# A block-sparse attention and SwiGLU kernel: queries loaded for both halves of the rows, constant masks, other landing times and ranks in its planner

## The chip, the core and the metric

One core of a Trainium2 chip runs the kernel. The engines named here are TensorE (PE, matmuls; PEld its weight loads), VectorE (DVE), ScalarE (ACT), GpSimd (POOL) and SyncE (SP), which only issues transfers. The metric is the time of one execution in microseconds (us) on the device; lower is better. A table of runs gives a median and its extremes, and one execution was profiled.

## What is computed

Attention over blocks of 32 positions, where a block sees its two neighbours, itself, the first and the last block and three sampled ones, and the first and last block see all. Its output, rows of 8 heads x 64, goes through a SwiGLU feed-forward network (FFN).

```python
B, H, S, D = 4, 8, 768, 64          # 24 blocks of 32
scores = (1 / sqrt(D)) * q @ k.T
mask = (abs(blk_i - blk_j) <= 1) | (blk_i == 0) | (blk_j == 0) | (blk_i == 23) | (blk_j == 23)
mask |= "kb in sampled_blocks[qb]"  # 3 sampled blocks for every block of queries
scores = where(mask, scores, -1e9)
attn = softmax(scores)              # exp(s - max) / (sum + 1e-9)
x = (attn @ v).transpose(0, 2, 1, 3).reshape(3072, 512)
g, val = x @ w_gate, x @ w_val      # 512 -> 1536
out = (g * sigmoid(g) * val) @ w_out  # 1536 -> 512
```

All tensors are fp32. q and k are drawn with a standard deviation of about 0.4, v with 0.1.

## The kernel before

**Tiling.** The 3072 rows are eight chunks of 384 rows, two for each batch: chunk 2b holds blocks 1 to 12 of batch b, chunk 2b+1 blocks 0, 23 and 13 to 22. A chunk has three tiles of 128 rows (four blocks). For every chunk come the attention blocks, then the FFN: 24 groups of 12 gate and value matmuls (p, L1462) and 12 groups of 9 for the output (po, L1508).

**Precision.** Chunk 0 is computed in fp32 while the weights are still on their way. From chunk 1 on, each fp32 operand is scaled by a power of two and split into two fp16 parts, high and low (ScalarE's L380, VectorE's L383), and a product is the sum of three fp16 products (two loops over high and low for the scores). The power of two comes from the sum of squares: ScalarE squares with a running sum (L391), TensorE adds over partitions, VectorE does the exponent arithmetic (pow2, L373 to L377).

**A block** (function `block`): scores qk (L1170) into PSUM, from the keys of its window (kst) and copied keys (kring, L1142); the masked maximum `top` (L682) on VectorE, exponentials (L1187 to L1190) on ScalarE, reciprocal, high and low half of the normalised weights pp (L380, L383), a transposing transfer to pts (L1215) issued by SyncE, and the product with v (L1229). `full_rows` does blocks 0 and 23 against all keys (qkf L962, pvf L1029).

**The queries** (function `load_q`). The host's qT holds each tile's queries as 128 rows, of which rows 64 to 127 are a copy of rows 0 to 63; a row holds 8 heads x 128 positions. A tile is loaded by two transfers of 64 rows (L881, on POOL's queue for batches 1 to 3, on SyncE's for batch 0), each taking every second head, so 128 partitions hold each head once. They are squared (L391), the norm is summed (nrm_q, L896), the high and low halves are written beside the raw tile in the staging buffer (`two`), and four transfers inside the chip (`spread`, L906, SyncE) write both halves into qs, so that each head is there for both halves of the partitions.

**Scales and masks.** The factor on the scores is (key scale) x (query scale) x 1/8. Since the scores in PSUM are still scaled, each tile makes three factors (es, L1095 to L1097) and a mask of its own, msk = dup x (a large negative number in the tile's scale), L1099. `top` adds it; dup counts duplicate key blocks.

**The order.** A `Plan` holds every step as a task: engine, its time in us, what it needs, the buffers it takes and uses, and for a step that issues transfers their time (`dma`). `order` is a list scheduler over a modelled clock: on each free engine it takes the waiting task with the lowest rank whose buffers are free. A transfer starts DMA_HEAD after its issue, queues behind others, and is taken to have landed DMA_TAIL after its end and no earlier than DMA_LATE after its issuing step. RANKS, a table of two bytes for each task, sets the ranks. The engines then run the steps in the planned order and wait on semaphores for what they need, so the plan sets the order and the chip the times. Rings of buffers: staging 4, qs 2, pp, pts and e 3 each, qk and pv 2 each in PSUM, FFN 4 in PSUM, keys kst 1.

```python
                if t.dma is not None:
                    start = max(queue.get(eng, 0.0), now + DMA_HEAD)
                    both = sum(max(0.0, q - start) if eng == "SP" else min(t.dma, max(0.0, q - start)) for e, q in queue.items() if e != eng)
                    queue[eng] = start + t.dma + both
                    t.end = max(queue[eng] + DMA_TAIL, t.end + DMA_LATE)
```

## Time and profile before

| what | value |
|---|---|
| median of 3 runs | 886.74 us |
| lowest, highest | 876.78, 895.16 us |
| the profiled execution, its own time | 888.1 us |
| its span (first to last instruction) | 886.3 us |
| mean granted TensorE clock | 0.940 |
| TensorE busy | 785.5 us (89%) |
| VectorE busy | 569.4 us (64%) |
| ScalarE busy | 513.2 us (58%) |
| GpSimd busy | 264.4 us (30%) |
| moved by transfers | 138.38 MB, 156 GB/s |

The page cuts the span into 40 equal slices of 22 us; a digit is a tenth of busy time, PEclk the granted clock in tenths.

```profile
PE   5778963599998959799799999999699999999998
DVE  6647868898897736667467657675477647851220
PEclk9878985889999889999999999999799999999999
DMA  8997879868564997669968786689959553652001
```

In the first ten slices VectorE is busy and TensorE has gaps; then TensorE is nearly always busy until the end. Transfers are nearly always under way up to the last tenth. A row of a group gives line, engine, operation, output and inputs, the count, busy time and mean time of one, and idle time of the engine ahead of it with what ended most of that. In the other views a row starts with a time from the span's start.

### The profile page before, as it was taken

The page shows a single profiled execution, that of the slowest core. Times are in us where ns is not written, and L with a number is a line of the kernel's source. Part 1 is how long each engine was busy: PE and PEld are TensorE (multiplying, and loading weights), DVE is VectorE, ACT ScalarE, POOL GpSimd, SP SyncE. Part 2 cuts the span into 40 slices and gives each one's busy share as a digit, 9 for nine tenths or more (in the row PEclk, how much of TensorE's full clock was granted, in tenths as well). Part 3 has the DMA queues.
Part 4 walks back from the last instruction along what each step waited for, and adds up shares of the span by engine and source line. Part 5 has one row for each costly group of instructions (what it writes and reads, how often), then busy time and mean ns, then how long its engine had stood idle before and what let it go on. Part 6 is the DMA issues. An engine that isn't in the chain of part 4 may idle for free.

```text
span 886.3 us, 24339 instructions
## 1 busy us (share of the span) xinstructions
PE 785.5 (89%) x9436; PEld 466.2 (53%) x9436; DVE 569.4 (64%) x1855; ACT 513.2 (58%) x1260; POOL 264.4 (30%) x371
## 2 busy tenths in 40 slices
PE   5778963599998959799799999999699999999998
PEld 4665542354565525465355646654366556655653
DVE  6647868898897736667467657675477647851220
ACT  4756465766688635578357556675366647652220
POOL 3423234561134312334124322332123311320220
PEclk9878985889999889999999999999799999999999
DMA  8997879868564997669968786689959553652001
GB/s 228 211 228 224 202 131 284 226 206 193 110 145 143 221 179 156 138 157 228 201 157 148 137 171 137 158 218 160 174 130 179 121 150 59 138 118 39 1 1 36
DMA packets 178083, 138.38 MB, mean 156 GB/s; under 512 B 138480, under 2 KB 141680, under 8 KB 177968
## 3 DMA queue, kind: packets, MB, share of 16 engines
q1 hardware_dynamic: 162704, 92.78, 49.6%
q0 software_dynamic: 11680, 37.76, 17.9%
q10 hardware_dynamic: 3584, 6.29, 2.4%
q8 instruction: 74, 1.21, 0.6%
q14 instruction: 41, 0.34, 0.1%
HBM read 80.68 MB, written 12.58 MB: 105 GB/s over the span
## 4 chain that ended last, share of the span: by engine, by line
PE 68%; DMA 20%; DVE 7%; issue 2%; ACT 1%; SPq 1%; POOL 0%; DVEq 0%; POOLq 0%; ACTq 0%
PE p L1462 33%; PE po L1508 14%; DMA pts<-pp 4%; PE qk L1170 4%; PE pv L1229 4%; PE po L1385 4%; PE p L1329 3%; DMA ptsf<-ppf 3%; DMA qs<-qraw 2%; DMA kst<-k 2%; DMA w1raw<-in_w_dram 2%; DMA w<-in_v_dram 1%; DVE w L413 1%; PE p L1339 1%; PE qkf L962 1%
## 5 line engine op out<-in xcount | busy, mean ns | idle before, releaser
L1462 PE MATMUL p<-xt,w 128*128 128x384 f16 x2016 | 344.4, 330 | 2.0 <-ACT xt L1245 1.4
L1462 PEld LDWEIGHTS <-w 128*128 128x128 f16 x2016 | 194.3, 99 | 135.6 <-issue 10.7
L1508 PE MATMUL po<-w,h 128*128 128x512 f16 x756 | 172.1, 384 | 0.0
L1483 POOL TENSOR_TENSOR h<-act,h 128x384 f16<-128x384 f32 x84 | 80.4, 960 | 269.4 <-ACT h L1480 269.0
L1151 POOL DMA_INDIRECT vring<-vd,vidx x76 | 74.5, 981 | 182.4 <-PE pv L1229 130.5
L1508 PEld LDWEIGHTS <-h 128*128 128x128 f16 x756 | 72.1, 99 | 94.7 <-issue 13.9
L1190 ACT ACTIVATE e<-e,nb,es 128x256 f32<-128x256 f32 x152 | 90.0, 593 | 2.5
L1466 ACT ACTIVATE act<-p,gsc 128x384 f32<-128x384 f32 x84 | 48.1, 576 | 60.2 <-PE p L1462 36.4
L383 DVE SCALAR_TENSOR_TENSOR pp<-e,rr,pp 128x256 f16<-128x256 f32 x152 | 72.1, 519 | 9.0 <-ACT pp L380 7.8
L380 ACT ACTIVATE pp<-e,rr 128x256 f16<-128x256 f32 x152 | 67.4, 498 | 17.8 <-DMA pts<-pp 11.0
L1469 DVE SCALAR_TENSOR_TENSOR act<-act,p 128x384 f32<-128x384 f32 x84 | 46.1, 548 | 47.8 <-ACT act L1466 45.5
L1229 PE MATMUL pv<-pts,vring 128*64 128x32 f16 (+1 forms) x2432 | 53.2, 194 | 22.1 <-DMA pts<-pp 16.7
L1480 ACT CAST h<-act 128x384 f16<-128x384 f32 x84 | 42.1, 506 | 51.4 <-DVE act L1472 51.1
L1229 PEld LDWEIGHTS <-vring 128*64 128x64 f16 x2432 | 48.0, 116 | 39.5 <-issue 33.1
L1472 DVE SCALAR_TENSOR_TENSOR act<-act,hs,p 128x384 f32<-128x384 f32 x84 | 51.3, 612 | 23.8 <-PE p L1462 21.4
L682 DVE CUSTOM_DVE_ANT_1 e<-qk,msk 128x256 f32<-128x256 f32 x152 | 57.2, 418 | 9.4 <-PE qk L1170 9.4
L1170 PEld LDWEIGHTS <-qs 128*32 128x32 f16 x2432 | 36.9, 102 | 32.7 <-issue 24.8
L1170 PE MATMUL qk<-kring,qs 128*32 128x160 f16 x1216 | 43.2, 248 | 6.0 <-DVE kring L1142 6.0
L1170 PE MATMUL qk<-kst,qs 128*32 128x96 f16 x1216 | 39.8, 218 | 9.3 <-ACT ef L984 3.8
L1142 DVE COPY kring<-kst 128x256 f16 x198 | 36.7, 245 | 7.9 <-PE qk L1170 6.7
L881 POOL DMA_DIRECT2D qraw<-in_q_dram x36 | 23.2, 648 | 52.3 <-DMA qs<-qraw 31.2
L1400 ACT ACTIVATE ot<-po,oc 128x512 f32<-128x512 f32 x21 | 14.3, 680 | 41.1 <-PE po L1508 41.1
(195 smaller groups left out, 1129.8 us busy)
## 6 DMA issues: line engine op xcount, KB each, us to landing
vring<-vd SPq DMA_DIRECT2D x76, 192.0 KB
w1raw<-in_w_dram SPq DMA_DIRECT2D x24, 512.0 KB
qs<-qraw SPq DMA_DIRECT2D x84, 128.0 KB
vfull<-vd POOLq DMA_DIRECT2D x12, 512.0 KB
w2raw<-in_w_dram SPq DMA_DIRECT2D x12, 512.0 KB
out_dram<-ot ACTq DMA_DIRECT2D x20, 256.0 KB
qraw<-in_q_dram POOLq DMA_DIRECT2D x36, 128.0 KB
kraw<-in_k_dram POOLq DMA_DIRECT2D x9, 512.0 KB
```

What stands on the lines that cost most here:

```text
L380: nc.scalar.activation(hi, src, AF.Copy, scale=scale)
L383: nc.vector.scalar_tensor_tensor(lo, src, scale, hi, op0=ALU.mult, op1=ALU.subtract)
L682: nc.vector.tensor_tensor_reduce(ev[:, g], stv[:, g], msk.unsqueeze(2).broadcast_to([P, 8, BLK]), scale=scale, scalar=-3.0e38 if scale > 0 ...
L1151: nc.gpsimd.indirect_dma_start(vf[0:96, 1, :], None, bt.vd, bass.IndirectOffsetOnAxis(ap=vidx[0:96, qb : qb + 1], axis=0))
L1170: nc.tensor.matmul(stv[u * BLK : (u + 1) * BLK, g, sl].rearrange("p s k -> p (s k)"), o.q[:, l, h // 2, h % 2, col : col + BLK], keys_of(h ...
L1190: nc.scalar.activation(ev[:, g], ev[:, g], AF.Exp, bias=nb_[:, g : g + 1], scale=o.es[:, 0:1], accum_out=c["rs"][:, g : g + 1],)
L1229: nc.tensor.matmul(pvv[hh * D : (hh + 1) * D, n % 2, j, 0 : 2 - l], vg[:, cc, l, 2 * j + hh, :], pq[:, g, 0 : 2 - l, cc, u, :], start=cc = ...
L1462: nc.tensor.matmul(t[:, 0:T], w_[:, f, m, k_, :], xt.tile[:, l, k_, :], start=i == 0, stop=i == 11)
L1466: nc.scalar.activation(get(act, f"act_{ci}_{f}"), pg.tile[:, 0:T], AF.Tanh, scale=c["gsc"][:, f : f + 1])
L1472: nc.vector.scalar_tensor_tensor(act.tile, act.tile, c["hs"][:, 1:2], pw.tile[:, 0:T], op0=ALU.mult, op1=ALU.mult)
L1483: nc.gpsimd.tensor_tensor(hv()[:, 1, :], act.tile, hv()[:, 0, :], op=ALU.subtract)
L1508: nc.tensor.matmul(po.tile, hv[:, l, ts_], wo16[:, f, m, :], start=f == 0 and i == 0, stop=f == NF - 1 and i == 2)
```

## The change

One load of 128 rows x 1024 columns (512 KB) brings a query tile, the copy of the rows too, so that both halves of the partitions hold all eight heads. The square runs on 64 rows of 1024 columns, since the other 64 are the same numbers; the high and low halves are made for all 128 rows and written straight into qs, and no transfer spreads them. So the square now takes the qs buffer, and its ScalarE output is a part of qs that is overwritten later.

The mask no longer has the tile's scale: -(2^100) x min(dup, 1), made once at the start. `top` waits for that constant, and the exponential for the tile's scale. The keys' scale is stored with factors of 1/8 and -1/8, and a tile's es is one instruction.

In the planner, transfers are taken to land later (DMA_TAIL, DMA_LATE and several `dma` times), a batch's loads of keys and values wait for the load two before and not one, and the table of ranks is another.

```diff
-DMA_HEAD, DMA_TAIL, DMA_LATE = 1.0, 0.5, 1.35
+DMA_HEAD, DMA_TAIL, DMA_LATE = 1.0, 1.6, 2.2
...
 RANKS = """
-    IETuJBIk6kKSJb4mySPIL0M1fjSfNBshHDi0NJ8kFCSMKsYmSS+nIrgqUjO5JIow8CwaGepHEzHvJ1ICXyOBFWMcvhL8NdUeGCNBODMyfinqA5
+    BbJbrbiv6LrBrIqtdK3nrhSzrrcQqunElqxOsJOjeLkokrF7k61zuo2oRrAwrOqyy6xlqseSmp8pr5ujNqk4op+lHHjqskurj7k+s++eXKnJos
...
-        "qs": (work, [P, 2, 2, 4, P], F16, 2),
+        "qs": (work, [P, 2, 4, 2, P], F16, 2),
...
-        v_.tensor_scalar(dup, dup, 1.0, None, op0=ALU.min)
-        v_.tensor_scalar(dupm, dup, -(2.0 ** 100), None, op0=ALU.mult)
+        v_.tensor_scalar(dupm, dup, 1.0, -(2.0 ** 100), op0=ALU.min, op1=ALU.mult)
...
-            loads.append(add("POOL" if b else "SP", 0.75 if b else 0.42, load, need + (loads[-1:] if b else []), rank, ...
+            loads.append(add("POOL" if b else "SP", 0.75 if b else 0.42, load, need + (loads[-2:-1] if b else []), rank, ...
...
-            sc["s"] = small_t([P, 2], f"{what}s", f"{what}s_{b}", 2)
+            sc["s"] = small_t([P, 4], f"{what}s", f"{what}s_{b}", 2)
             pow2(m, sc["s"][:, 0:1], sc["s"][:, 1:2], 1, f"{what}{b}", 0 if what == "k" else 8)
+            if what == "k":
+                for i, x in enumerate((0.125, -0.125)):
+                    nc.vector.tensor_scalar(sc["s"][:, 2 + i : 3 + i], sc["s"][:, 1:2], x, None, op0=ALU.mult)
...
-                                    use=pi + ([] if f0 else [bt.ks]), dma=1.25))
+                                    use=pi + ([] if f0 else [bt.ks]), dma=1.5 if b else 2.5))
...
         def load():
-            raw = get(st, f"qraw_{si}")[:, 0:512]
-            for hh in range(2):
-                sl = slice(hh * D, (hh + 1) * D)
-                (nc.gpsimd if b else nc.sync).dma_start(
-                    raw[sl, :].rearrange("p (j q) -> p j q", j=4),
-                    qT[b, sub, sl, :].rearrange("p (j t q) -> p t j q", j=4, t=2)[:, hh],
-                )
-
-        def two():
-            return st.tile.bitcast(F16)[:, 1024:2048].rearrange("p (l n) -> p l n", l=2)
+            (nc.gpsimd if b else nc.sync).dma_start(get(st, f"qraw_{si}"), qT[b, sub])
+
+        def part(l):
+            return o.q[:, l].rearrange("p j t q -> p (j t q)")
 
         def square():
+            o.q = get(qs, f"qs_{si}")
             o.acc = small_t([P, 1], "qacc", f"qacc_{si}")
-            sumsq(st.tile[:, 0:512], o.acc, two()[:, 0, :])
+            nc.scalar.activation(part(0)[0:D].bitcast(BF16), st.tile[0:D], AF.Square, accum_out=o.acc[0:D])
...
-        def spread():
-            q_ = get(qs, f"qs_{si}")
-            for hh in range(2):
-                for to in range(2):
-                    nc.sync.dma_start(
-                        q_[to * D : (to + 1) * D, hh].rearrange("p l j q -> p (l j q)"),
-                        two()[hh * D : (hh + 1) * D].rearrange("p l n -> p (l n)"),
-                    )
-
-            o.q = q_.rearrange("p t l j q -> p l j t q")
-
-        t = add("POOL" if b else "SP", 1.3 if b else 1.25, load, need, rank, take=[st], dma=1.4, behind=...)
+        t = add("POOL" if b else "SP", 0.75 if b else 0.4, load, need, rank, take=[st], dma=1.7, behind=...)
         q_load.append(t)
-        t = add("ACT", 0.66, square, [t], rank, use=[st])
+        t = add("ACT", 1.15, square, [t], rank, take=[qs], use=[st])
         t = add("PE", 0.1, norm, [t], rank, take=[n])
         o.scaled = add("DVE", 0.6, scale, [t], NORM, use=[n])
-        t = add("ACT", 0.72, lambda: hi_part(two()[:, 0, :], st.tile[:, 0:512], o.siq[:, 0:1]), [o.scaled], rank, use=[st])
-        t = add("DVE", 0.75, lambda: lo_part(two()[:, 1, :], st.tile[:, 0:512], o.siq[:, 0:1], two()[:, 0, :]), [t], rank, use=[st])
-        o.done = add("SP", 2.45, spread, [t], rank, take=[qs], use=[st], dma=2.45)
+        t = add("ACT", 1.15, lambda: hi_part(part(0), st.tile, o.siq[:, 0:1]), [o.scaled], rank, use=[st, qs])
+        o.done = add("DVE", 1.3, lambda: lo_part(part(1), st.tile, o.siq[:, 0:1], part(0)), [t], rank, use=[st, qs])
...
-            def scale(o=o, si=si, sparse=sparse):
-                o.es = small_t([P, 3], "es", f"es_{si}")
-                nc.vector.tensor_scalar(o.es[:, 0:1], bt.ksc["s"][:, 1:2], o.siq[:, 1:2], 0.125, op0=ALU.mult, op1=ALU.mult)
-                nc.vector.tensor_scalar(o.es[:, 2:3], bt.ksc["s"][:, 1:2], o.siq[:, 1:2], -0.125, op0=ALU.mult, op1=ALU.mult)
-                nc.vector.tensor_scalar(o.es[:, 1:2], bt.ksc["s"][:, 0:1], o.siq[:, 0:1], -8e9, op0=ALU.mult, op1=ALU.mult)
-                o.msk = small_t([P, 4, 8], "msk", f"msk_{si}", 4)
-                nc.vector.tensor_scalar(
-                    o.msk[:, 0 : len(sparse), :], dup[:, sparse[0] : sparse[-1] + 1, :], o.es[:, 1:2], None, op0=ALU.mult
-                )
-
-            tsc = add("DVE", 0.85, scale, [o.scaled, bt.ksc_t, t_dup], r0)
+            def scale(o=o, si=si):
+                o.es = small_t([P, 2], "es", f"es_{si}")
+                nc.vector.tensor_scalar(o.es, bt.ksc["s"][:, 2:4], o.siq[:, 1:2], None, op0=ALU.mult)
+
+            tsc = add("DVE", 0.2, scale, [o.scaled, bt.ksc_t], r0)
...
-        vl = add("SP", 1.2 if new else 0.45, values, bt.v_done + v_read[slot], rank, dma=1.05)
+        vl = add("SP", 1.2 if new else 0.45, values, bt.v_done + v_read[slot], rank, dma=1.9 if new else 1.15)
...
-        a = in_turn("top", "DVE", 0.75, top, [a, tsc, full_exp[0]], rank, take=[e], use=[qk])
-        a = in_turn("exp", "ACT", 1.5, power, [a], rank, use=[e])
+        a = in_turn("top", "DVE", 0.75, top, [a, t_dup, full_exp[0]], rank, take=[e], use=[qk])
+        a = in_turn("exp", "ACT", 1.5, power, [a, tsc], rank, use=[e])
...
-        a = add("SP", 1.27, turn, [a], rank, take=[pts], use=[pp], dma=1.35)
+        a = add("SP", 1.27, turn, [a], rank, take=[pts], use=[pp], dma=1.5)
```

In the full rows the tile's es takes the place of a factor of their own (esf, L946).

How the order moves is shown at three places. A row is a line of the kernel, an operation, its output and its inputs (the number at a name's end counts the buffers handed out), its shape, and how many alike follow one another. Lines of the changed kernel are about 25 lower: L380 is L378 there, L391 L389 or L889, L1187 L1162, L1190 L1165, L1215 L1190, L1142 L1117, L1462 L1437.

First, ScalarE ahead of chunk 1's feed-forward part. w are the weights being squared and split, e and pp a block's exponentials and normalised weights (the number after the name is the block), act_0 is chunk 0's first gate.

```order
L380 ACTIVATE pp_17_2464<-e_17_2031,rr_17_2424 128x256 x2
L380 ACTIVATE pp_18_2471<-e_18_2083,rr_18_2278 128x256 x2
L391 ACTIVATE wsq_2_2478,oacc<-w_99 128x512
L1245 CAST xt_120<-pv_15_2153 128x4x64
L1187 ACTIVATE nb_20_2495<-mx_20_2486,es_2285 128x2
L1190 ACTIVATE e_20_2485,rs_20_2494<-e_20_2485,nb_20_2495,es_2285 128x256 x2
L380 ACTIVATE w_97<-w_97,wsc 128x512
L380 ACTIVATE w_98<-w_98,wsc 128x512
L458 CAST w_97<-w_97 128x512
L1343 ACTIVATE act_0_2563<-p_0_2334,gsc_2516 128x384
```

Before, blocks 17 to 20 stand among the weights and ahead of chunk 0's gates. After the change the same blocks stand here:

```order
L1162 ACTIVATE nb_17_2586<-mx_17_2570,es_1403 128x2
L1165 ACTIVATE e_17_2569,rs_17_2585<-e_17_2569,nb_17_2586,es_1403 128x256 x2
L1162 ACTIVATE nb_18_2700<-mx_18_2626,es_1403 128x2
L1165 ACTIVATE e_18_2625,rs_18_2699<-e_18_2625,nb_18_2700,es_1403 128x256 x2
L378 ACTIVATE pp_17_2748<-e_17_2569,rr_17_2739 128x256 x2
L1162 ACTIVATE nb_19_2790<-mx_19_2745,es_2214 128x2
L1165 ACTIVATE e_19_2744,rs_19_2789<-e_19_2744,nb_19_2790,es_2214 128x256 x2
L389 ACTIVATE k_1_0_2527,kacc_2803<-kraw_0_2524 128x2x512
L378 ACTIVATE pp_18_2874<-e_18_2625,rr_18_2751 128x256 x2
L889 ACTIVATE qs_2879,qacc_2880<-qraw_2227 64x1024
```

The blocks follow one another, with squares of keys and queries of batch 1 between them; chunk 0's gates stand ahead of them all.

Second, SyncE's queue in the first half of batch 1, before. pts are the transposing transfers, vring the values of a block's window.

```order
L1215 DMA_TRANSPOSE pts_7_4569<-pp_7_4488 128x8x128
L1148 DMA vring_112<-vd_114 96x1024
L1215 DMA_TRANSPOSE pts_8_4646<-pp_8_4560 128x8x128
L906 DMA qs_4697<-qraw_3770 64x1024 x4
L1215 DMA_TRANSPOSE pts_9_4787<-pp_9_4654 128x8x128
L1148 DMA vring_110<-vd_114 96x1024
L1148 DMA vring_111<-vd_114 96x1024
L1215 DMA_TRANSPOSE pts_10_4856<-pp_10_4735 128x8x128
```

The same place after the change:

```order
L1190 DMA_TRANSPOSE pts_7_4603<-pp_7_4540 128x8x128
L1123 DMA vring_112<-vd_114 96x1024
L1190 DMA_TRANSPOSE pts_8_4623<-pp_8_4564 128x8x128
L1190 DMA_TRANSPOSE pts_9_4754<-pp_9_4625 128x8x128
L1123 DMA vring_110<-vd_114 96x1024
L1123 DMA vring_111<-vd_114 96x1024
L1190 DMA_TRANSPOSE pts_10_4862<-pp_10_4820 128x8x128
```

Only the four spreading transfers between the blocks 8 and 9 are gone.

Third, VectorE where batch 3's keys come in. es and msk are the scale and mask of the first query tile, kring the copied keys of a block, hs the normalisation of the feed-forward part of the chunk before.

```order
L1096 TENSOR_SCALAR es_10884<-ks_10536,siq_10870 128x1
L1097 TENSOR_SCALAR es_10884<-ks_10536,siq_10870 128x1
L1099 TENSOR_SCALAR msk_10888<-dup,es_10884 128x32
L383 SCALAR_TENSOR_TENSOR qraw_10655<-qraw_10655,siq_10870 128x512
L1139 COPY kring_108<-kst_10651 128x8x32
L1140 COPY kring_108<-kst_10651 128x8x32
L1142 ISA
L1142 COPY kring_108<-kst_10651 128x8x32
```

Twelve rows later comes the first row of the normalisation (L1435, hs). After the change:

```order
L1410 TENSOR_REDUCE hs_10766<-xn_10748 128x1
L1412 TENSOR_SCALAR hs_10766<-hs_10766 128x1
L1413 TENSOR_SCALAR hs_10766<-hs_10766 128x1
L1414 TENSOR_SCALAR hs_10766<-hs_10766 128x1
L1417 TENSOR_SCALAR gsc_10771<-wsc,vs_6102 128x12
L1419 SCALAR_TENSOR_TENSOR oc_10773<-vs_6102,hs_10766 128x1
L1471 SCALAR_TENSOR_TENSOR oc_10773<-oc_10773,osc 128x1
L1444 SCALAR_TENSOR_TENSOR act_0_10776<-act_0_10776,p_0_10716 128x384
L1447 SCALAR_TENSOR_TENSOR act_0_10776<-act_0_10776,hs_10766,p_0_10734 128x384
L1444 SCALAR_TENSOR_TENSOR act_1_10791<-act_1_10791,p_1_10753 128x384
L1447 SCALAR_TENSOR_TENSOR act_1_10791<-act_1_10791,hs_10766,p_1_10778 128x384
L1114 COPY kring_107<-kst_10551 128x8x32
```

The copies of keys now stand behind the normalisation and the first two gates of that feed-forward part.

On TensorE the list has 16,822 rows after the change and 16,825 before, on VectorE 1,927 and 1,988, on ScalarE 818 in both, on GpSimd 394 and 393, and on SyncE 303 and 323.

More of the change, by code (lines that the diff above doesn't have):

```diff
@@ L564, in load @@
                 (nc.gpsimd if b else nc.sync).dma_start(raws[i][1](), src[b, i * 256 : (i + 1) * 256, :].rearrange("(t p) n -> p t n", p=P))
-            loads.append(add("POOL" if b else "SP", 0.75 if b else 0.42, load, need + (loads[-1:] if b else []), rank, behind=loads[0] if i else None, take=[] if i else bufs + parts[:1],
+            loads.append(add("POOL" if b else "SP", 0.75 if b else 0.42, load, need + (loads[-2:-1] if b else []), rank, behind=loads[0] if i else None, take=[] if i else bufs + parts[:1],
                              use=[buf] if i and b else [], dma=2.1 if b else 1.6))
@@ L648, in put @@
                     )
-                done.append(add("SP", 0.43, put, los, rank, use=parts[i : i + 1], dma=1.45))
+                done.append(add("SP", 0.43, put, los, rank, use=parts[i : i + 1], dma=1.55))
             bt.all_lo += los
@@ L942, in full_rows @@
                           use=vbuf[i : i + 1] if i else [], dma=1.85))
-        def scale():
-            es[0] = small_t([P, 1], "esf", f"esf_{b}")
-            nc.vector.tensor_scalar(es[0], bt.ksc["s"][:, 1:2], o.siq[:, 1:2], 0.125, op0=ALU.mult, op1=ALU.mult)
-        tsc = add("DVE", 0.2, scale, [bt.ksc_t, o.scaled], rank)
         pvs = []
@@ L1181, in top @@
             c["mx"] = small_t([P, 2], "mx", f"mx_{nq}")
-            masked_top(ev, qk.tile.rearrange("p (g s k) -> p g s k", g=2, k=BLK), o.msk[:, n, :], c["mx"])
+            masked_top(ev, qk.tile.rearrange("p (g s k) -> p g s k", g=2, k=BLK), dupm[:, qb, :], c["mx"])
         def power():
```

155 lines of the change are left out of this document (77 added, 78 removed).

## The prediction

> **What bounds the kernel now.** I read the page's span and the shares of the chain that ended last first, then the table of four stretches, then the waits of TensorE.
>
> ```profile
> span 886.3 us, 24339 instructions
> PE 68%; DMA 20%; DVE 7%; issue 2%; ACT 1%; SPq 1%; POOL 0%; DVEq 0%; POOLq 0%; ACTq 0%
> core 0: us, PE busy (x) PEld busy (x) DVE busy (x) ACT busy (x) POOL busy (x), PEclk, DMA share, GB/s
> 0.00:76.00 76.00, 52.66 (x897) 44.99 (x897) 48.27 (x172) 48.15 (x137) 29.49 (x73) 0.87 1.02 230
> 76.00:232.30 156.30, 121.80 (x1113) 68.78 (x1114) 126.52 (x330) 97.63 (x234) 54.92 (x95) 0.84 0.79 199
> 232.30:812.00 579.70, 540.89 (x7033) 313.90 (x7032) 380.61 (x1331) 351.61 (x862) 169.06 (x192) 0.97 0.73 153
> 812.00:886.30 74.30, 70.13 (x397) 38.56 (x394) 14.05 (x24) 15.84 (x28) 10.94 (x12) 1.00 0.05 15
> ```
>
> Two thirds of the chain is TensorE and a fifth is transfers. The stretches are cut where chunk 1's feed-forward part (FFN 1) starts, 232.3, and where chunk 7's starts, 812.0. From 232.3 on TensorE is the bound: it is busy 540.9 of 579.7 us, and idle 38.8. The last stretch is feed-forward work of chunk 7 alone and stays as it is. Ahead of 232.3 the kernel is bound by VectorE, busy 126.5 of 156.3 us (0.81); weights are split and chunk 1's blocks are done there.
>
> These are TensorE's waits behind 232 us: the total, how many, and the longest.
>
> ```profile
> PE nrm_q L896 <- ACT qraw L391: 11.9, 3, 6.9
> PE qk L1170 <- DVE kring L1142: 6.0, 2, 5.6
> PE pv L1229 <- DMA pts<-pp: 5.4, 5, 1.8
> PE pv L1229 <- DMA vring<-vd,vidx: 3.6, 2, 1.9
> PE xn L1431 <- ACT sqx L1425: 2.6, 1, 2.6
> PE pvf L1029 <- DMA ptsf<-ppf: 2.4, 4, 1.1
> PE qkf L962 <- DMA qs<-qraw: 0.9, 1, 0.9
> ```
>
> They make 32.8 of the 38.8 us. The largest is the norm of a query tile, which waits for ScalarE's square. The chain (start, length, what) and SyncE's queue show where the longest of the three comes from, and the windows what it does to the clock:
>
> ```profile
> 305.07 5.22 SPq L906 DMA_DIRECT2D qs<-qraw  x4
> 309.83 7.72 DMA qs<-qraw
> 318.49 10.98 DMA pts<-pp
> 329.82 0.20 ACT qraw L391
> 320.00:330.00 10.00, 3.20 (x44) 1.53 (x43) 1.60 (x7) 1.84 (x7) 1.82 (x2) 0.81 1.14 180
> ```
>
> SyncE issues four spreading transfers, 5.2 us in its queue; the spread is 7.7 us under way; a transposing transfer behind it, pts, takes 11.0; ScalarE, held by that, comes to the next tile's square only at 329.8. From 320 to 330 the transfer engines are full (share 1.14), TensorE works 3.2 of ten us, and its clock falls to 0.81.
>
> **The change part by part: the query tile.** The rows of the tile's steps behind 232 us give durations (min/median/max ns); below them are the size of one spreading transfer, the 128x1024 square of keys, and the load of a tile where it stood on the chain.
>
> ```profile
> L906 SPq DMA_DIRECT2D qs<-qraw x64: 462/591/1587, 250.7 to 764.3; - x64
> L881 POOL DMA_DIRECT2D qraw<-in_q_dram x30: 617/637/673, 256.2 to 720.6; - x30
> L380 ACT ACTIVATE qraw<-qraw,siq x16: 705/715/724, 233.8 to 759.6; 128x512 f16<-128x512 f32 x16
> L383 DVE SCALAR_TENSOR_TENSOR qraw<-qraw,siq x16: 739/751/1430, 236.3 to 761.7; 128x512 f16<-128x512 f32 x16
> L391 ACT ACTIVATE qraw<-qraw x15: 613/629/632, 263.6 to 724.5; 128x512 bf16<-128x512 f32 x15
> qs<-qraw SPq DMA_DIRECT2D x84, 128.0 KB
> L391 ACT ACTIVATE k<-kraw 128x1024 bf16<-128x1024 f32 x9 | 9.4, 1047 | 1.3 <-DMA kraw<-in_k_dram 1.3
> 366.88 5.26 DMA qraw<-in_q_dram
> ```
>
> Removed: four issues of 0.591 us per tile on SyncE, 64 behind 232 us, 38 us of its queue, and 512 KB of transfer per tile. Of what stood behind them in that queue, the pts transfers matter. Added: the load brings 512 KB in one transfer instead of 256 KB in two, so a tile moves 512 KB and not 768. POOL issues once, 0.637 us less per tile. The load's time has no row: it lies between the 5.26 us that the load of half the bytes took on the chain and twice that, 10.5; I take 7, nearer to the lower row, since rows of the same tile are contiguous now and the spreads no longer run beside it. It stands ahead of its use by a tile where a staging buffer is free, and then costs nothing; with that cover gone it costs up to 5 us for each tile that is late.
>
> ScalarE's square goes from 128x512 to 64x1024: between 0.629 (half the rows for twice the columns, same work) and 1.047 (the keys' row of the same width); I take 1.05, the row with equal columns, +0.42. The high half goes from 128x512 to 128x1024: from 0.715 to twice it, 1.43; I take 0.715 + 0.42 = 1.13. So +0.84 us for each of 16 tiles, 13 us on an engine that is busy 351.6 of 579.7 us: covered. VectorE's low half is between 0.751 and 1.50; I take 1.50, +0.75.
>
> The rows that the query path makes others wait behind are these (behind 232 us, engine's own or queue's waits):
>
> ```profile
> POOL qraw L881 <- DMA qs<-qraw: 30.2, 7, 7.3
> SPq L906 <- PE qk L1170: 22.2, 4, 10.8
> SPq L906 <- DVE qraw L383: 17.6, 6, 8.9
> ACT qraw L391 <- DMA qraw<-in_q_dram: 18.4, 6, 5.1
> ```
>
> POOL's 30.2 goes: no spread holds the staging buffer, VectorE's low half frees it. SyncE's 22.2 and 17.6 go, and pts and vring transfers no longer stand behind them. The 22.2 is the wait for a free qs buffer (two of them); it moves to ScalarE's square, which takes the buffer now. What is queued behind a square that waits is all of ScalarE: exponentials, high halves, gates of the FFN. In the new order squares stand later, about where the scores of the older tile are through, so I cost this at nothing and keep 22.2 as its bound.
>
> Of the three waits of nrm_q I take 11.9 to 3: the 6.9 was the spread and the pts behind it; the other two, 5.0 together, are partly the load's. I take 9 us, 0.9 for qkf, and of the 11.4 us of pts, pvf and vring waits half, 5.4, since SyncE's queue and the transfer engines are emptier. Together 15.
>
> *A rule weighed.* The Trainium skill, page "DMA: Bandwidth & Descriptors", section "Anatomy of one DMA — SWDGE (gpsimd) path", gives about 2.0 us and the bytes at 436 GB/s for one DMA on that path; for 128 KB that is an estimate of 2.3 us, for 512 KB of 3.2. By it a tile would save only about 1.4 us of transfer time, the three nrm_q waits 4 us and not 9, and the time would be 869, inside the forecast. The pieces of 5.26 and 7.72 us above do not agree: the engines were full there.
>
> **Masks and scales.**
>
> ```profile
> L1099 DVE TENSOR_SCALAR msk<-dup,es 128x32 f32<-128x32 f32 x17 | 4.7, 274 | 0.6
> L1099 DVE TENSOR_SCALAR msk<-dup,es 128x16 f32<-128x16 f32 x4 | 4.3, 1086 | 0.1
> L1095 DVE TENSOR_SCALAR es<-ks,siq 128x1 f32<-128x1 f32 x21 | 4.4, 209 | 0.4
> ```
>
> A tile loses a mask (0.274, or 1.09 in four tiles) and two of three es, 0.42: 0.69 us of VectorE. Against +0.75 for the low half that is nothing, and VectorE is busy 380.6 of 579.7 us. The maximum no longer waits for the tile's scale, only the exponential does.
>
> **Order.**
>
> ```profile
> 232.28 1.95 PE p L1462 x12
> ```
>
> A group of 12 gate matmuls takes 1.95 us (the first on the chain). The first scores of batches 2 and 3 stood behind 4 and 3 such groups of the chunk before, 7.8 and 5.9 us; now behind 9 and 7, 17.6 and 13.7. The copies of keys into kring stand behind the FFN's first gates on VectorE, not ahead of the normalisation. So kring's 6.0 goes to 1 (its longest, 5.6, is that place) and xn's 2.6 to 1: 6.6. The FFN matmuls that cover this are only moved: TensorE's list has 16,822 rows for 16,825. Two batch loads of 512 KB may now be under way at once; POOL's list has one row more, and I cost it at nothing: they come half a chunk ahead.
>
> So idle behind 232.3 us falls by 15 + 6.6, 22 us, to 17. The clock rises with it: 540.9 us at 0.97 is 525 at full clock; at 0.98 it is 535 to 536, 5 less, of which I take 4, since the stretch of 0.81 above goes and others stay. Sum of this stretch: −26.
>
> **Ahead of FFN 1** the order is another one: weights are decoded and chunk 0's FFN done first, then ten blocks of chunk 1 (13 to 22) stand with no FFN between. VectorE's rows up to block 13, counted with their groups' means, leave 86 us at 76.0, and the ten blocks 46 more. At the stage's 0.81 the first part ends at 76 + 106 = 182, at 0.9 at 171.5; the ten blocks take 46/0.81 = 57. FFN 1 would start at 239 or 229; I take the middle, 234, +2. ScalarE's work in the ten blocks is no less:
>
> ```profile
> L1190 ACT ACTIVATE e<-e,nb,es 128x256 f32<-128x256 f32 x152 | 90.0, 593 | 2.5
> L1190 ACT ACTIVATION_READ_ACCUMULATOR e<-e,nb,es 128x1 f32 x152 | 28.4, 187 | 0.0
> L1187 ACT ACTIVATE nb<-mx,es 128x2 f32<-128x2 f32 x76 | 21.9, 288 | 17.8 <-DVE mx L682 17.2 <-issue 0.5
> L380 ACT ACTIVATE pp<-e,rr 128x256 f16<-128x256 f32 x152 | 67.4, 498 | 17.8 <-DMA pts<-pp 11.0 <-issue 4.5 <-DVE rr L677 1.3
> 130.00:150.00 20.00, 7.04 (x206) 6.12 (x205) 16.76 (x51) 11.45 (x35) 6.28 (x9) 0.54 1.04 277
> ```
>
> A block is 2 × (0.593 + 0.187 + 0.498) + 0.288 = 2.84 us, ten 28.4; 14 high halves of weights and keys at 0.715, 10.0; three query tiles and three key squares, about 9.5; copies about 5: 53 us. It fits into 57 only if ScalarE is busy 0.93 of it, and in the whole stage it is busy 97.6 of 156.3, 0.62. This is the weakest term; I keep −10 to +30 for it.
>
> *Another rule weighed.* The Trainium skill, page "TensorE: Matmul & The Clock Gate", section "Part 1: The HAM clock gate", says that TensorE drops to half clock after an idle window of about 3.4 us. The row of 130 to 150 us agrees in kind (busy 7.0 of 20, clock 0.54). By it the ten blocks' scores and products (0.57 and 0.62 us in the planner's costs) take twice as long; with three blocks in flight a third of those 12 us would show, and the sum would be 868, inside the forecast. It speaks against the change.
>
> **The sum** is −26 + 2 = −24 against the profiled execution, whose own time is 888.1 us (span 886.3 and 1.8 around it): 864.1. The median of the runs shown, 886.7, is 1.4 below it, inside their spread of 876.8 to 895.2; I take nothing off.
>
> **Rivals.**
> *Everything gains.* The ten blocks run at VectorE's 0.9 and start FFN 1 at 222 (−10), and remaining waits fall to 9, not 17 (−8): 888.1 − 26 − 18 = 844, or about 850 with one of them. For it speaks that VectorE's work is no more than before; against it ScalarE's 0.93.
> *The wait for queries only moves.* ScalarE's square waits for the older tile's scores (22.2 us in 4, longest 10.8, was hidden in SyncE's queue) or for a load of 10.5 us, and the norm is as late as before. Then only the 6.6 of kring and xn stay, with 1 to 2 of clock: −8, 880. For it speaks that 18.4 us of ScalarE's waits were for the load already; against it the emptier transfer engines.
> *The other side: the ten blocks.* ScalarE keeps its rate of 0.62 there: 53/0.62 = 85 us, not 57: +28, and FFN 1 starts at 262. With −26 behind it that is 892, with the −8 of the rival above 910. It decides against the change where ScalarE's rate is below about 53/81 = 0.65. For it: block after block waits on maximum, exponential, pts, with no FFN between; against it: before, ScalarE was held there by VectorE's decoding, which is now done.
>
> **How the numbers follow.** Two per cent is about what a measurement of this kernel can tell from no change: 869.0 and 904.5. Forecast, 854 to 876 about 864: 0.43, of it 0.33 below 869. Everything gains, near 850: 0.15, faster. The wait moves, near 880: 0.20, within. The ten blocks, 892 to 910: 0.22, of it 0.10 within and 0.12 slower. Faster 0.48, same 0.40, slower 0.12. The range: 888.1 − 10 − 34 − 1.4 = 843 leaves little below, 842; above, 896 leaves out about 0.16 of the last rival.
>
> **What would show it.** Right: FFN 1's first matmul near 234 us; nrm_q waits under 4 us behind it; no qs transfers; SyncE's pts no longer behind anything of queries; kring at most 1; TensorE idle near 17 us between FFN 1 and chunk 7's FFN; clock 0.98. Wrong: ScalarE's square with long waits for a score or a load; FFN 1 behind 250 us; or new waits for vring or pts, which the order alone does not show.

## The result

The changed kernel takes 853.3 us (median of 4 runs, 848.5 to 857.6), the kernel before 886.2 beside it: a ratio of 0.966, 95% interval 0.956 to 0.976. It is faster by 3.4%. In a second group of runs the ratio was 0.961 (0.951 to 0.971). The forecast was 864, with 842 to 896 for its range.

The profiled execution of the changed kernel took 853.7 us, with a span of 851.9. Its chain, and its stretches cut at the same places of the work as before (FFN 1's first matmul at 221.5, chunk 7's FFN at 776.6; columns as in the prediction's table):

```profile
PE 77%; DMA 10%; DVE 8%; issue 2%; ACT 2%; SPq 1%; POOL 0%; ACTq 0%; DVEq 0%; POOLq 0%
0.00:76.00 76.00, 58.02 (x927) 48.58 (x928) 52.78 (x178) 55.91 (x152) 28.13 (x65) 0.87 0.97 266
76.00:221.50 145.50, 113.00 (x1082) 62.41 (x1081) 117.27 (x306) 96.12 (x224) 56.31 (x99) 0.86 0.74 184
221.50:776.60 555.10, 538.66 (x7030) 310.28 (x7030) 382.92 (x1281) 363.34 (x859) 162.22 (x177) 0.98 0.71 153
776.60:851.90 75.30, 70.81 (x401) 38.92 (x398) 15.30 (x31) 15.85 (x28) 10.93 (x12) 0.99 0.04 15
```

Transfers had a fifth of the chain and now have a tenth. Against 886.3 the span is 34.4 us shorter: 10.8 ahead of FFN 1 (232.3 to 221.5), 24.6 from there to chunk 7's FFN (579.7 to 555.1), and 1.0 lost in the last stretch. In the third stretch TensorE is busy 538.7 of 555.1 us; its idle time fell from 38.8 to 16.4 us, its clock rose from 0.97 to 0.98. What it still waits for there (total, times, longest):

```profile
PE p L1437 <- ACT xt L1220: 4.2, 2, 3.7
PE pv L1204 <- DMA pts<-pp: 2.6, 2, 2.0
PE p L1437 <- DVE act L1444: 2.1, 2, 1.9
PE pvf L1010 <- DMA ptsf<-ppf: 1.6, 1, 1.6
PE qk L1145 <- DVE kring L1117: 1.4, 1, 1.4
```

No wait of a query norm is left in this stretch (11.9 us before), none for a query's transfer, none of xn; kring is 1.4 and not 6.0.

One caution for reading the stages. The time of the kernel before varies from 867 to 895 us over all runs shown here, and the execution profiled first, 888.1 us, is among the longer ones. Its second profiled execution, 871.0 us, beside which the changed kernel was run again, had other stretches. These are the third stretches of that pair:

```profile
226.30:794.74 568.44, 538.45 (x7034) 312.56 (x7033) 381.35 (x1331) 351.56 (x863) 169.30 (x192) 0.98 0.74 156
218.20:770.10 551.90, 536.37 (x7029) 309.33 (x7029) 384.66 (x1281) 363.35 (x859) 163.19 (x177) 0.99 0.71 154
```

Here the third stretch gained 16.5 us and not 24.6, and FFN 1 came 8.1 earlier. Single profiles of one kernel differ by up to 11 us in a stretch; the ratios below rest on more runs. Ratios leave disturbed runs out and medians do not, so the two can stand apart, by 1.5 per cent in one case below.

### The profile page after: what moved, and what is told of

It reads as the page before. It is cut to its first block, busy times and chain, and to the rows that moved or that the text cites. A ratio compares the mean times of both kernels' runs of the same rounds, so it can differ in the third digit from the quotient of the medians.

```text
span 851.9 us, 23999 instructions
## 1 busy us (share of the span) xinstructions
PE 780.5 (92%) x9436; PEld 460.2 (54%) x9436; DVE 568.3 (67%) x1795; ACT 531.2 (62%) x1260; POOL 257.6 (30%) x353
## 4 chain that ended last, share of the span: by engine, by line
PE 77%; DMA 10%; DVE 8%; issue 2%; ACT 2%; SPq 1%; POOL 0%; ACTq 0%; DVEq 0%; POOLq 0%
PE p L1437 37%; PE po L1483 18%; PE qk L1145 5%; PE pv L1204 4%; DMA pts<-pp 4%; PE p L1304 3%; PE po L1360 3%; DMA kst<-k 2%; DMA w1raw<-in_w_dram 2%; DMA vring<-in_v_dram,vidx 2%; DVE w L413 1%; DVE w L415 1%; PE qkf L943 1%; PE pv L842 1%; PE p L1314 1%
## 5 line engine op out<-in xcount | busy, mean ns | idle before, releaser
L1437 PE MATMUL p<-xt,w 128*128 128x384 f16 x2016 | 346.0, 330 | 7.6 <-ACT xt L1220 4.2
L1437 PEld LDWEIGHTS <-w 128*128 128x128 f16 x2016 | 194.0, 99 | 141.4 <-issue 16.2
L1165 ACT ACTIVATE e<-e,nb,es 128x256 f32<-128x256 f32 x152 | 90.0, 593 | 2.5
L1441 ACT ACTIVATE act<-p,gsc 128x384 f32<-128x384 f32 x84 | 48.3, 576 | 67.4 <-PE p L1437 35.2
L378 ACT ACTIVATE pp<-e,rr 128x256 f16<-128x256 f32 x152 | 67.2, 497 | 17.8 <-DMA pts<-pp 6.9
L684 DVE CUSTOM_DVE_ANT_1 e<-qk,dupm 128x256 f32<-128x256 f32 x176 | 66.3, 418 | 15.3 <-PE qk L1145 8.9
L1447 DVE SCALAR_TENSOR_TENSOR act<-act,hs,p 128x384 f32<-128x384 f32 x84 | 51.3, 611 | 17.8 <-PE p L1437 15.3
L1117 DVE COPY kring<-kst 128x256 f16 x198 | 40.7, 269 | 14.8 <-PE qk L1145 14.0
L1145 PEld LDWEIGHTS <-qs 128*32 128x32 f16 x2432 | 33.8, 96 | 22.4 <-issue 15.2
L1145 PE MATMUL qk<-kring,qs 128*32 128x160 f16 x1216 | 41.0, 233 | 2.7 <-DVE kring L1117 1.4
L1145 PE MATMUL qk<-kst,qs 128*32 128x96 f16 x1216 | 37.7, 208 | 4.3 <-issue 1.4
L1360 PE MATMUL po<-w,h 128*128 128x512 f32 x72 | 35.2, 633 | 2.5 <-DVE w L415 2.5
```

The source lines that it names most:

```text
L378: nc.scalar.activation(hi, src, AF.Copy, scale=scale)
L684: nc.vector.tensor_tensor_reduce(ev[:, g], stv[:, g], msk.unsqueeze(2).broadcast_to([P, 8, BLK]), scale=scale, scalar=-3.0e38 if scale > 0 ...
L1145: nc.tensor.matmul(stv[u * BLK : (u + 1) * BLK, g, sl].rearrange("p s k -> p (s k)"), o.q[:, l, h // 2, h % 2, col : col + BLK], keys_of(h ...
L1165: nc.scalar.activation(ev[:, g], ev[:, g], AF.Exp, bias=nb_[:, g : g + 1], scale=o.es[:, 0:1], accum_out=c["rs"][:, g : g + 1],)
L1360: nc.tensor.matmul(po.tile, h_f32(f)[:, ts_], wo[:, f + 1, :], start=f == LAST[0], stop=f == LAST[-1])
L1437: nc.tensor.matmul(t[:, 0:T], w_[:, f, m, k_, :], xt.tile[:, l, k_, :], start=i == 0, stop=i == 11)
```

## The experiments

The rank table is made for one set of costs: with any cost changed, the list scheduler gives another order everywhere. So most experiments keep an order that is given: the table holds the place of each step in one of the two kernels, and `order` takes from each engine's list the next step (in short):

```python
heads = [x[0] for x in lists.values() if x and can(x[0])]   # can: needs and buffers are there
if not heads:                                               # else the first that can
    heads = [next((t for t in x if can(t)), None) for x in lists.values()]
t = min([h for h in heads if h is not None], key=lambda t: (t.rank, t.no))
```

"The new order" is the changed kernel's, "the old order" that of the kernel before. A ratio is the time of a run's kernel over that of the kernel before in the same group of runs. No run shows what the planner would make of the old path with the new landing times, or of the new path with the old ones, and the two batch loads at once were not tried alone. Two theories stand at the start: A, the new way of the queries brings the gain; B, the new order does.

**The old query path in the new order.** Load, square, halves and spread are those of the kernel before; the masks are the new ones.

```diff
-            nc.scalar.activation(part(0)[0:D].bitcast(BF16), st.tile[0:D], AF.Square, accum_out=o.acc[0:D])
+            sumsq(st.tile[:, 0:512], o.acc, two()[:, 0, :])
...
+        o.done = add("SP", 2.45, spread, [t], rank, take=[qs], use=[st], dma=2.45)
```

> The changed kernel in its own order, with the old way of the queries put back: two loads of 64 rows, square and halves of 128x512, four spreading transfers right behind the low half. If the gain is the query path's (theory A): the queue of SyncE and the transfer engines are loaded again, nrm_q, qkf and pts waits return, about 18 us behind FFN 1's start, and what chunk 0 gained ahead of it, up to 10: 871 to 881 us. If the gain is the order's (theory B, which hides the spread as well): 855 to 862.

Measured: 881.2 us, ratio 1.010 (1.003 to 1.017). The third stretch, and TensorE's largest waits in it:

```profile
223.30:803.39 580.09, 543.66 (x7029) 312.37 (x7029) 376.48 (x1283) 350.14 (x859) 170.63 (x194) 0.97 0.73 155
PE nrm_q L859 <- ACT qraw L349: 8.9, 4, 3.3
PE pv L1182 <- DMA pts<-pp: 7.1, 4, 3.4
PE qk L1123 <- DMA qs<-qraw: 6.2, 4, 2.9
PE qkf L921 <- DMA qs<-qraw: 5.3, 2, 4.9
```

This order without its path is worth nothing; it is a little slower than before. Scores and full rows now wait for the spread itself, 11.5 us, where they waited 0.9 before: the new order leaves no time for it.

**The new query path in the old order.** The changed kernel's steps, masks too, in the places of the kernel before (the table of ranks is described here, not printed).

```diff
-    RANKS: places in the new order
+    RANKS: places in the old order, without the spreads
...
-                need + (loads[-2:-1] if b else [])
+                need + (loads[-1:] if b else [])
```

> The changed kernel's query path, masks and scales in the order of the kernel before (same steps in the same places on each engine, the spreads left out, batch loads one after the other). Theory A: the waits of nrm_q fall from 11.9 to about 3 here too, kring's 6.0 and xn's 2.6 stay: 860 to 868 us. Theory B: the waits stay or come back at other places: 876 to 886.

Measured: 879.7 us, ratio 1.008 (0.999 to 1.016). The third stretch, three of TensorE's waits in it, and ScalarE's for the square:

```profile
224.80:809.21 584.41, 544.21 (x7034) 314.35 (x7033) 390.00 (x1290) 366.92 (x865) 160.29 (x177) 0.97 0.67 144
PE pv L1163 <- DMA pts<-pp: 10.1, 8, 2.4
PE nrm_q L853 <- ACT qs L848: 9.2, 7, 1.6
PE qk L1104 <- DVE kring L1076: 7.1, 2, 3.8
ACT qs L848 <- PE qk L1104: 21.1, 13, 3.8
```

The new path in this order is worth nothing either. Its squares now wait 21.1 us for scores that free a qs buffer, nearly the 22.2 us that SyncE's queue waited before, and ScalarE's queue stands behind them. Neither theory holds alone.

**A third qs buffer in that run.**

```diff
-        "qs": (work, [P, 2, 4, 2, P], F16, 2),
+        "qs": (work, [P, 2, 4, 2, P], F16, 3),
```

> The new query path in the old order once more, with a third qs buffer, so that ScalarE's square finds a free one. Theory C: in the old order the square's wait for the buffer (21.1 us on ScalarE in 13 waits, in the run with two buffers) ate what the path gives, since it stood in the way of the exponentials; then the stretch from FFN 1 to chunk 7's FFN falls from 584 to 568 us or less and nrm_q's waits from 9.2 to 4 or less. Theory D: the old order itself (kring, pts and xn waits, nrm_q close behind the load) keeps it at 578 to 586 with any number of buffers.

Measured: 860.4 us, ratio 0.981 (0.973 to 0.988). The third stretch, TensorE's largest wait in it, and the one that is left to ScalarE's squares for data or buffers:

```profile
222.20:783.17 560.97, 537.67 (x7033) 311.88 (x7032) 386.95 (x1286) 364.04 (x862) 159.52 (x177) 0.98 0.70 150
PE pv L1163 <- DMA pts<-pp: 12.0, 5, 4.5
ACT qs L848 <- DMA qraw<-in_q_dram: 6.6, 4, 3.5
```

One buffer takes 23.4 us off the stretch. The wait for scores is gone from ScalarE and nrm_q from TensorE's waits; those for pts stay. Theory C holds: the buffer's wait is what kept the new path from gaining in the old order. The changed kernel, with two buffers and the new order, took 846.1 us in the same group of runs, 14 us less (ratio 0.961).

**A third qs buffer in the kernel before**, nothing else changed.

> The kernel before in its own order with a third qs buffer and nothing else. The new query path with three buffers in this order was 0.981. If that was the path's (the missing transfers): no change here, ratio 0.993 to 1.005, since the wait for the buffer stood in SyncE's queue and only moved the spreads. If it was the buffer's (the 22.2 us that SyncE's queue waited for it held back pts and vring transfers): ratio 0.975 to 0.988, the wait of the spreads for the scores gone.

Measured: 874.9 us against 875.5, ratio 0.990 (0.985 to 0.996). That is between the two expectations. The third stretch was 563.0 us in its profile, and SyncE's wait for scores was gone, while the spreads stayed; FFN 1 started at 231.5:

```profile
231.50:794.50 563.00, 537.34 (x7034) 312.10 (x7033) 382.29 (x1331) 351.39 (x863) 168.70 (x192) 0.98 0.74 158
SPq L865 <- DVE qraw L342: 17.8, 5, 10.1
```

So the buffer alone is worth about one per cent by the ratio, hardly anything by the medians, and the path with the buffer about two (on another chip). In the third stretch the profiles with three buffers are only 2 us apart, 563.0 with the spreads and 561.0 without; they differ ahead of FFN 1, 231.5 against 222.2. How much of the gain in the old order is the path's, and how much the buffer's, is therefore open.

**A third qs buffer in the changed kernel.**

> The changed kernel in its own order with a third qs buffer. In the old order the third buffer was worth 23 us between FFN 1 and chunk 7's FFN. In the new order squares stand behind the scores that free the buffer, and ScalarE waited 1.7 us for it: ratio 0.957 to 0.970, no difference to the changed kernel. If the buffer still holds something the waits don't show, 0.945 to 0.957.

Measured: 854.4 us, against 884.0 for the kernel before in that group; ratio 0.982 (0.962 to 1.001); the two medians stand as 0.967 to 1. The ratio lies outside both expectations, the medians inside the first. The interval holds the 0.966 without the buffer, though not the 0.961, and shuts out the gain of the second expectation; the third stretch is 561.8 us, no shorter than the 555.1 and 551.9 with two buffers. So nothing shows that the new order lacks one.

**Idle spreads in the changed kernel.** Four transfers of 128 KB for each tile, from qs into a buffer that nobody reads, behind the low half. Their results are not used, but a tile's qs buffer isn't free until they have read it.

```diff
+                    nc.sync.dma_start(
+                        d[to * D : (to + 1) * D, hh].rearrange("p l j q -> p (l j q)"),
+                        o.q[hh * D : (hh + 1) * D, to].rearrange("p j t q -> p (j t q)"),
+                    )
```

> The changed kernel with four more transfers of 128 KB for each query tile, from qs into a buffer that nobody reads, issued by SyncE right behind the low half: the load of the old spreads on SyncE's queue and the transfer engines, without a reader that waits for them. If SyncE's queue and the full engines made the spreads dear (my working gave pts, pvf and vring 5.4 us of the gain): the stretch behind FFN 1's start rises from 555 to 565 or more, with pts and vring waits. If it was the spread's own length between the load and the scores: 555 to 559.

Measured: 874.0 us, ratio 0.998 (0.994 to 1.001), against 846.1 and 0.961 for the changed kernel in the same group. The third stretch, TensorE's waits, and two of ScalarE's; the last two lines are TensorE's waits for the same transfers in the changed kernel of that group:

```profile
220.60:795.12 574.52, 543.39 (x7030) 313.18 (x7030) 380.69 (x1281) 363.30 (x859) 162.80 (x177) 0.97 0.77 162
PE pv L1177 <- DMA pts<-pp: 11.1, 8, 4.9
PE pvf L983 <- DMA ptsf<-ppf: 7.8, 4, 4.0
PE pv L1177 <- DMA vring<-vd,vidx: 2.6, 2, 1.9
ACT act L1414 <- DMA dump<-qs: 10.7, 1, 10.7
ACT qs L850 <- PE qk L1118: 1.7, 2, 1.3
PE pvf L1010 <- DMA ptsf<-ppf: 5.5, 5, 3.2
PE pv L1204 <- DMA pts<-pp: 2.7, 1, 2.7
```

The first expectation holds, but the size was the surprise: transfers whose results nobody reads cost 28 us, nearly all that the change brought. TensorE is idle 31.1 us in the stretch and not 15.5, and 13.3 of these 15.6 us are the longer waits for pts, ptsf and vring. It is also busy 7.0 us longer for the same work, at a clock of 0.97 and not 0.99. The buffer that the idle transfers hold is not the reason: squares wait 1.7 us for scores and never for an idle transfer (dump<-qs). One wait does end with such a transfer, ScalarE's 10.7 us ahead of an output's issue and a gate, and TensorE lost 4.0 us behind it. In the first profile of the changed kernel ScalarE waited 10.4 us at the same place, for kst, and TensorE lost 1.9; so this wait accounts for about 2 us. Why the issue waits there at all is open.

**The same with 4 KB in each of the four transfers**, and **the same 512 KB in one transfer.**

```diff
-                        d[to * D : (to + 1) * D, hh].rearrange("p l j q -> p (l j q)"),
+                        d[to * D : (to + 1) * D, hh].rearrange("p l j q -> p (l j q)")[:, 0:32],
...
+            nc.sync.dma_start(d.rearrange("p t l j q -> p (t l j q)"), o.q.rearrange("p l j t q -> p (l j t q)"))
```

> The run with idle spreads once more, four transfers for each query tile at the same places in SyncE's queue and with as many rows, but of 4 KB each and not 128. If the 28 us by which the idle spreads slowed the changed kernel were their place in SyncE's queue (theory E: what stands behind them there is issued later): the time stays near that run, ratio to before 0.985 to 1.00. If they were the bytes on the transfer engines (theory F): ratio 0.960 to 0.972.

> The run with idle spreads once more, with the same 512 KB for each tile in one transfer and not in four. Theory E (four issues in SyncE's queue): most of the loss goes, ratio 0.965 to 0.98. Theory F (bytes on the transfer engines): the loss stays, 0.99 to 1.00.

Measured: 859.6 us (ratio 0.984, 0.970 to 0.999) and 869.1 (0.991, 0.983 to 0.998), beside 854.4 for the changed kernel with its third buffer, all on one chip. Against that run the four small transfers cost 5 us, within its spread of 853.6 to 862.1, and the bytes in one transfer 15 by the medians, about 8 by the ratios (0.991 against 0.982). The second is what theory F expected; the first has an interval that reaches into both expectations. So the bytes on the transfer engines are a part of the 28 us, at most about half by these runs. Neither part alone makes the whole, and how issue and bytes share the rest isn't settled: the groups ran on different chips, and the ten runs with one transfer spread from 859 to 873.

**Masks back.** A mask and three factors for each tile again, the maximum waiting for the scale, in the new order.

```diff
-        a = in_turn("top", "DVE", 0.75, top, [a, t_dup, full_exp[0]], rank, take=[e], use=[qk])
+        a = in_turn("top", "DVE", 0.75, top, [a, tsc, full_exp[0]], rank, take=[e], use=[qk])
```

> The changed kernel in its own order with a mask and three factors for each query tile again, the maximum waiting for the tile's scale. 0.69 us more of VectorE for each of 21 tiles, 14.5 us in all. If VectorE's work behind FFN 1's start is covered and only the three tiles ahead of it show (my working): 852 to 857 us. If the wait of the maximum for the scale is what counted (rival): kring or score waits return, 860 to 866.

Measured: 855.0 us, ratio 0.977 (0.970 to 0.984). The third stretch:

```profile
227.80:776.97 549.17, 533.61 (x7029) 308.56 (x7029) 391.15 (x1332) 363.39 (x859) 161.97 (x177) 0.99 0.72 155
```

VectorE works 8 us more there, and nothing waits for it: the stretch is no longer than in the changed kernel, and the span is 852.4 against 851.9. FFN 1 started at 227.8, 6 us later, of which the stretch gave as much back. The time is what was expected for covered work. But by the ratios the run stands a per cent or more behind the changed kernel (0.977 against 0.961 and 0.966), with intervals that just overlap: a small effect of the masks ahead of FFN 1 is neither shown nor excluded.

**The first stage's old order** in the changed kernel: all steps up to chunk 1's blocks stand in the old order within the places that they have in the new one.

> The changed kernel with the order of the kernel before for all steps up to chunk 1's blocks (chunk 0, weights, batch 0, chunk 1), each engine's other steps where they were. FFN 1 starts at 221.5 us in the changed kernel and at 232.3 before. If the new order of that stage brought the 10.8 us (theory B for this stage): FFN 1 starts near 232 and the time is 861 to 867. If the missing spreads and the shorter queue brought them (theory A): FFN 1 starts at 219 to 223 and the time is 850 to 856.

Measured: 891.3 us, ratio 1.021 (1.014 to 1.028), outside of both expectations. FFN 1 started at 253.3. TensorE's largest waits from chunk 0's FFN to there:

```profile
PE p L1273 <- ACT w L415: 15.5, 2, 12.9
PE pv L1163 <- DMA pts<-pp: 13.8, 4, 5.6
```

ScalarE's weights come late among batch 1's steps: the mixture is worse than either order. Behind it the stretch is 556.7 us, as in the changed kernel. The run shows that 30 us can hang on this stage's order; what the old order itself costs there it does not tell.

**The two kernels again**, on one chip with the idle spreads.

> The kernel before, for its stages on the chip on which the others of this group run. Its TensorE time from FFN 1's start to chunk 7's should be near 580 us as in the first profile. If the earlier start of FFN 1 in the runs with one part undone (223 to 225 us) was the chip's, FFN 1 starts near 224 us here; if the change's, near 232.

> The changed kernel beside the others of this group. All theories: a ratio near 0.966, FFN 1's start to chunk 7's near 555 us.

Measured: 871.0 us in one run, and 846.1 (ratio 0.961, 0.951 to 0.971). FFN 1 started at 226.3 and 218.2, between what was expected for the first: a part of the earlier starts in the runs with one part undone was the chip's or the execution's.

## Why the prediction was right, and where not

- **TensorE is the bound from FFN 1 on, and its idle time is the gain.** Right. Idle time was to fall from 38.8 to 17 us and is 16.4; in the second pair of profiles it fell from 30.0 to 15.5. The clock was taken from 0.97 to 0.98 and did that, but TensorE's busy time fell by 2.2 us where 4 were taken.
- **Single terms.** nrm_q was to fall by 9 and qkf by 0.9, and both went wholly, by 12.8. Pts, pvf and vring were to go from 11.4 to 6 and went to 4.2. Kring and xn were to lose 6.6 and lost 7.2. Kring was to be at most 1 and is 1.4. The waits for xt (4.2) and act (2.1) were not in the sum, and took 5 us of it back. Together 22.4 us of idle time, and with 2.2 us less of TensorE's busy time 24.6 against 26. That these sizes fit so closely is partly luck of the pair: in the second one nrm_q fell from 10.3 to nothing and kring from 4.0 to 1.5, but pts, pvf and vring only from 8.8 to 8.2, and the stretch gained 16.5.
- **The wait for a qs buffer, costed at nothing.** Right for this order, and only for it. ScalarE's waits of squares for scores in the changed kernel:

```profile
ACT qs L889 <- PE qk L1145: 1.7, 2, 1.3
```

In the old order it was 21.1. The rival "the wait for queries only moves" is what happens without the new order, and the third buffer shows that it is the buffer. POOL's wait of 30.2 us, which was to go, became one of 17.8 for VectorE's low half, which now frees the staging buffer; it cost nothing here.
- **The terms do not add.** The sum gave 15 to the path and 6.6 to the order as if each came alone. The runs with one of them gave 1.008 and 1.010; together they gave 0.966. This is the step that the prediction's total hid: the order makes room for squares that take qs, and the path takes away the spreads for which the order leaves no room.
- **What the spreads cost.** The prediction put 9.9 us on the waits of the queries themselves and 5.4 on the load that the spreads lay on SyncE's queue and the transfer engines. The idle spreads, which no query waits for, cost 28 us in the new order. The old path there was only about 1.2 per cent slower than that (1.010 against 0.998, two groups of runs). So the load was mis-sized for the new order, where it is the larger part. It is no constant: in the old order with three buffers the stretch was 563.0 us with the spreads and 561.0 without.
- **The steps' durations.** The changed kernel's rows:

```profile
L889 ACT ACTIVATE qs<-qraw x16: 1040/1056/1057, 253.0 to 703.7; 64x1024 bf16<-64x1024 f32 x16
L378 ACT ACTIVATE qs<-qraw,siq x16: 1132/1136/1151, 263.2 to 725.7; 128x1024 f16<-128x1024 f32 x16
L381 DVE SCALAR_TENSOR_TENSOR qs<-qraw,siq,qs x16: 1264/1278/1284, 264.9 to 727.0; 128x1024 f16<-128x1024 f32 x16
```

Square and high half were taken as 1.05 and 1.13 us and are 1.056 and 1.136; the low half was taken as 1.50 and is 1.28. ScalarE's 12 us more (363.3 against 351.6) are covered, as was said. The load was taken as 7 us, beside an estimate of 3.2. In the second profile of the changed kernel the median from issue to landing is 5.6 us for 512 KB, and 4.4 for one of the two loads of 128 KB in the kernel before beside it. ScalarE's squares wait 0.8 us for loads in this stretch, where they waited 18.4. The prediction called the engines full beside its 5.26 us of an earlier load; their share from 366 to 372 us was 0.73, and only beside the spread of 7.72 us was it above 1.
- **The start of FFN 1: the term that was off most.** It was put at 234, with −10 as its lower end, and is 221.5: 10.8 us gained where 2 were to be lost. These 12.8 us are more than the 10.4 by which the profiled execution, 853.7 us, beat the forecast of 864.1. The two parts, up to block 13's maximum and from there to FFN 1:

```profile
76.00:158.60 82.60, 70.88 (x355) 38.02 (x354) 75.34 (x167) 51.19 (x116) 39.83 (x71) 0.93 0.67 193
158.60:221.50 62.90, 42.12 (x728) 24.39 (x728) 41.92 (x140) 44.94 (x108) 16.47 (x28) 0.77 0.84 171
```

The first part was to end at 171.5 to 182 and ended at 158.6. VectorE had done 52.8 us at 76.0 and not 48.3, its rows from there to block 13 were 75.3 us and not 86, and it was busy 0.91 of the time, where the prediction took the middle of 0.81 and 0.9. The ten blocks took 62.9 us against 57. ScalarE's work in them was 44.9 us and not 53, at a rate of 0.71; the rival that feared 0.62 was nearer in the rate than the 0.93 of the forecast, with too much work. The rival "everything gains" had FFN 1 at 222 and, with one of its two parts, about 850 us, which is what came. Its reason held only for the first part: in the ten blocks VectorE is busy 0.67 of the time and not 0.9. How the 10.8 us divide between path and order is open. FFN 1 started at 226.3 to 232.3 in three profiles with old path and old order, at 222.2 and 224.8 with the new path alone, at 223.3 with the new order alone, at 215.6 to 221.5 in six with both, and at 227.8 in the one with both and the old masks: some 5 us for each would fit, but profiles of one kernel differ by as much.
- **The clock rule.** The last part of that stage, and a product of scores and values in it and late in the kernel:

```profile
200.00:221.50 21.50, 6.48 (x194) 6.12 (x195) 13.08 (x38) 14.48 (x34) 3.96 (x5) 0.50 1.13 214
202.96 1.03 PE L1204 MATMUL pv<-pts,vring 128*64 128x64 f16 x32 [5.00 <-DMA pts<-pp]
764.21 0.68 PE L1204 MATMUL pv<-pts,vring 128*64 128x64 f16 x32
```

TensorE works 6.5 of 21.5 us there, its clock is 0.50, and the product takes 1.03 us and not 0.68. The Trainium skill, page "TensorE: Matmul & The Clock Gate", section "Part 1: The HAM clock gate", has half clock behind idle windows, and this agrees. But the product had waited 5.0 us for its pts: there the transfer set the pace. Whether any of the 4 us that the prediction worked out from the rule showed elsewhere in the ten blocks, no run tells.

## What to carry to other kernels

A step whose result takes a buffer later, on another engine's queue, moves the wait for that buffer to that engine: count the buffers and see what stands behind the new waiter before the transfers that go are booked as a gain. A path and the order around it are one change: each alone gave nothing here, so a term-by-term sum can be right in its total although its parts do not add up one by one. And transfers whose results nobody reads are not free where transposing transfers share their queue, and gathers the transfer engines.

## What was not expected of the hardware

Four idle transfers of 128 KB inside the chip for each of 21 tiles, 11.0 MB in 870 us, slowed the changed kernel by 28 us (846.1 to 874.0), while the engines' mean share in the long stretch was only 0.71 without and 0.77 with them. The mean gives no sign of it: TensorE's waits for pts went from 2.7 to 11.1 us.
